# One fp32 kernel on one core: the last two thirds of its instruction order written out as a list, some low halves moved to VectorE, the first loads reordered

## Chip, cores, metric

One core of a Trainium2 chip. The metric is the device time of one execution in microseconds. Engines are named as in the profile: PE is TensorE's matmuls, PEld its weight loads, DVE is VectorE, ACT is ScalarE, POOL is GpSimd, SP is SyncE.

## What is computed

The input x is 2 x 3008 x 256. A real part of a two-dimensional Fourier transform is followed by two gated layers, all in fp32.

```python
def _attn_ref(x):
    X = np.fft.fft(x, axis=1)
    X = np.fft.fft(X, axis=2)
    return X.real.astype(np.float32)

def _moe_ref(x, w_in, w_out):            # w_in 256 x 2048, w_out 2048 x 256
    h = x @ w_in
    relu6 = np.clip(h + 3.0, 0.0, 6.0)
    g = h * relu6 / 6.0
    return (g @ w_out).astype(np.float32)

def _moe2_ref(x, w_gate, w_val, w_out, rms_g):   # 256 x 1536, 256 x 1536, 1536 x 256
    rms = np.sqrt(np.mean(x * x, axis=-1, keepdims=True) + 1e-06)
    xn = x / rms * rms_g
    g = xn @ w_gate
    silu = g * (1.0 / (1.0 + np.exp(-g)))
    val = xn @ w_val
    return (silu * val @ w_out).astype(np.float32)
```

The weights arrive on the device as 64-bit words and are decoded there.

## The kernel before

**Arithmetic.** TensorE works in a format with fewer bits than fp32, so each operand is split into a high half (a copy by ScalarE, which rounds) and a low half (the difference, by `sub` at line 184, on POOL throughout). A product is three matmuls (`PASSES`): high x high, high x low, low x high.

**Transform.** For batch 0 the input is loaded in three pieces (`load_x`, tiles J0, J1, B0), folded by symmetry with sums and differences on VectorE (`sums`, `parts`, `fold`; low halves on POOL), and multiplied with cosine and sine matrices that are loaded as fp16 pairs (`load_raw`) and cast (`conv_mat`). `pmm` and `xmm` are these matmuls (378 columns), `evac` and `evac_x` take the result to the tiles PQX0 and X1, partly by DMA. Batch 1 is folded later (`late_fold`), split (`late_split`), given its matrices by DMAs on POOL's queue (`late_mat`) and multiplied in four groups (`group`) while layer 1 runs. The transform along the 256 columns is multiplied into layer 1's weights: `dec_win` decodes a chunk of w_in and `wmm` multiplies it with `dmat`; `dec_wout` decodes a chunk of w_out. `split_pq` makes the high and low halves of a block of 502 columns of the data.

**Layer 1** is 96 items (6 blocks of 502 columns, 16 chunks of the hidden size; `item1`). An item has eight steps, each on one engine:

1. TensorE, 6 matmuls into two PSUM banks E and O (line 449), out of two pairs of banks that rotate;
2. VectorE, one operation on E (line 453);
3. VectorE, two operations, E + t and t - O (455, 456);
4. ScalarE, two relus (461);
5. VectorE, two operations that read both banks for the last time (464);
6. ScalarE, the high half (467), tiles HI0 and HI1 in turn;
7. POOL, the low half, 128 x 1004 (185), tiles LO0 and LO1 in turn;
8. TensorE, 12 matmuls into four accumulator banks (481); the last of a block adds a step that takes them to a y1 tile.

**Layer 2** is 144 items (12 half blocks of 502 columns, 12 chunks): `in2` with 12 matmuls (608), a sigmoid on ScalarE (610) and two products on VectorE (612, 613); `mid2` with the high half on ScalarE (619) and the low half on POOL; `out2` with 6 matmuls (632). Ahead of a half block stand the RMS steps (`rms_steps`: a square on ScalarE, some fifteen operations on VectorE with three Newton steps, two matmuls). Its weights are loaded in 18 halves (`load_w2`), decoded by one operation on ScalarE and four on VectorE and split (`conv_w2`, lines 175 to 182 and 528); four halves go to HBM and come back later (`take_w2`).

**Order.** Each engine has one queue and runs it in order. All steps from the loads to layer 1's item 35 stand in a list, `STEPS`: each word names a task (the table `TASKS`) or an item, and each time a word occurs the next step of that task is issued; a yield in the code ends a step. This part stands under `tc.manual_schedule()`, which keeps it as written. From item 36 on a loop (`item`) issues the items with fixed distances, and side tasks at fixed places (`LATE`, `at`); this part is outside `manual_schedule`, so the framework's scheduler may order its instructions.

## Time and profile before

| | |
|---|---|
| median of 3 runs | 1177.63 us (1174.83 to 1177.73) |
| the profiled execution | 1175.49 us, span 1173.7 us |
| mean granted TensorE clock | 0.972 |
| TensorE busy | 1081.5 us (92% of the span), 4572 matmuls |
| VectorE busy | 850.3 us (72%), 1204 instructions |
| ScalarE busy | 500.7 us (43%) |
| POOL busy | 510.1 us (43%) |
| moved by DMA | 47.22 MB, mean 40 GB/s |

The profile is of one execution; matmul ends are modelled, so a busy share of TensorE is not its share of peak speed, and the pace at which matmuls start says more. Busy time counts each engine alone: two engines that are both below full can still hold each other up, and which one does is read stage by stage. A granted clock of 1.00 is 2.4 GHz; the lower level, 1.2 GHz, is 0.50.

### The profile page before, as it was taken

The numbers are of one execution on the slowest core, as the hardware profiler recorded it, in microseconds if no ns is written. First come the engines' busy times: TensorE is split into PE (matmuls) and PEld (weight loads), VectorE is DVE, ScalarE is ACT, GpSimd is POOL, SyncE is SP. The second block draws the span as 40 slices with busy tenths as digits, with TensorE's granted clock in tenths as the row PEclk, the third lists the DMA queues.
The fourth block names the chain that finished last, engine by engine and source line by source line (L and its number), as shares of the span: only waits on it lengthen the run. The fifth ranks groups of instructions, "written<-read, shape, count | busy, mean of one in ns | idle before, by whom it ended". The sixth has DMA issues, their size and how long they took to land.

```text
span 1173.7 us, 12674 instructions
## 1 busy us (share of the span) xinstructions
PE 1081.5 (92%) x4572; PEld 876.8 (75%) x4572; DVE 850.3 (72%) x1204; ACT 500.7 (43%) x754; POOL 510.1 (43%) x311
## 2 busy tenths in 40 slices
PE   4778777889999989988999999999999999999998
...
DMA packets 18896, 47.22 MB, mean 40 GB/s; under 512 B 3914, under 2 KB 6986, under 8 KB 17946
## 3 DMA queue, kind: packets, MB, share of 16 engines
...
## 4 chain that ended last, share of the span: by engine, by line
PE 59%; DVE 25%; issue 6%; ACT 4%; POOL 4%; DMA 2%; SPq 0%; DVEq 0%; POOLq 0%; ACTq 0%
PE acc L632 15%; PE E L608 14%; PE O L608 14%; PE acc L481 10%; DVE R L464 5%; DVE T L453 3%; DVE E L455 2%; PE O L449 2%; PE E L449 2%; DVE O L456 2%; POOL LO L185 1%; ACT R L461 1%; DVE c_p L182 1%; DVE c_p L177 1%; DMA J<-in_x 1%
## 5 line engine op out<-in xcount | busy, mean ns | idle before, releaser
L185 POOL TENSOR_TENSOR LO<-R,HI 128x1004 fp32r<-128x1004 f32 x96 | 233.3, 2435 | 198.3 <-ACT HI L467 189.0
L481 PE MATMUL acc<-HI,B 128*128 128x502 f32 x768 | 256.7, 401 | 4.8 <-ACT YB L496 2.2
L612 DVE TENSOR_TENSOR R<-T,E 128x502 f32<-128x502 f32 x144 | 97.4, 676 | 186.0 <-ACT T L610 183.7
L185 POOL TENSOR_TENSOR HI<-R,HI 128x502 fp32r<-128x502 f32 x87 | 115.3, 1325 | 223.8 <-ACT HI L619 223.1
L481 PEld LDWEIGHTS acc<-HI,B 128*128 128x128 f32 x768 | 149.0, 195 | 38.8 <-ACT YB L496 2.6
L467 ACT CAST HI<-R 128x1004 fp32r<-128x1004 f32 x96 | 99.0, 1033 | 151.9 <-PE acc L481 80.0
L481 PE MATMUL acc<-LO,B 128*128 128x502 f32 x384 | 154.6, 402 | 4.5 <-POOL LO L185 4.4
L608 PE MATMUL E<-J,B 128*128 128x502 f32 x576 | 147.5, 391 | 1.1 <-DVE R L612 1.1
L608 PE MATMUL O<-J,A 128*128 128x502 f32 x576 | 147.5, 390 | 1.0 <-ACT A L528 0.6
L610 ACT ACTIVATE T<-E 128x502 f32<-128x502 f32 x144 | 84.5, 588 | 133.7 <-PE E L608 133.5
L185 POOL TENSOR_TENSOR LO<-R,LO 128x502 fp32r<-128x502 f32 x57 | 76.2, 1337 | 145.9 <-ACT LO L619 145.9
L608 PEld LDWEIGHTS O<-J,A 128*128 128x128 f32 x576 | 108.6, 189 | 24.9 <-DVE R L613 1.2
L449 PE MATMUL E<-J,A 128*128 128x502 f32 x288 | 88.1, 418 | 41.9 <-DVE R L464 32.2
L608 PEld LDWEIGHTS E<-J,B 128*128 128x128 f32 x576 | 108.4, 189 | 24.4 <-DVE R L612 2.0
L613 DVE TENSOR_TENSOR R<-R,O 128x502 f32<-128x502 f32 x144 | 97.2, 676 | 11.3 <-DVE R L612 0.5
L449 PEld LDWEIGHTS E<-J,A 128*128 128x128 f32 x288 | 54.7, 198 | 63.1 <-DVE R L464 42.1
L619 ACT CAST HI<-R 128x502 fp32r<-128x502 f32 x87 | 53.1, 612 | 112.9 <-DVE R L613 112.9
L461 ACT ACTIVATE R<-E,c_three 128x502 f32<-128x502 f32 x96 | 65.3, 680 | 77.5 <-DVE E L455 66.6
L481 PEld LDWEIGHTS acc<-LO,B 128*128 128x128 f32 x384 | 74.8, 195 | 24.7 <-POOL LO L185 9.5
L449 PE MATMUL O<-J,A 128*128 128x502 f32 x288 | 86.7, 412 | 5.0 <-DVE A L233 2.6
L632 PE MATMUL acc<-HI,B 128*128 128x502 f32 x354 | 89.9, 391 | 0.4 <-POOL HI L185 0.4
L464 DVE SCALAR_TENSOR_TENSOR R<-R,E 128x502 f32<-128x502 f32 x96 | 64.5, 672 | 28.2 <-ACT R L461 28.1
...
## 6 DMA issues: line engine op xcount, KB each, us to landing
...
```

Source lines behind the costliest of these rows:

```text
L185: eng.tensor_tensor(o, a, b, op=ALU.subtract)
L449: T.matmul(bk[:, :BL], a[:, lw, eo, fs], j[:, eo, lx], start=(n == 0), stop=(n == 2))
L461: S.activation(x, bk[:, :BL], AF.Relu, bias=c3)
L464: V.scalar_tensor_tensor(x, x, 6.0, bk[:, :BL], op0=ALU.min, op1=ALU.mult)
L467: S.copy(hi, r)
L481: T.matmul(acc[k][:, :BL], w[:, lw, f % 4, d * P:(d + 1) * P], (hi, lo)[lx][:, hf * BL:(hf + 1) * BL], start=(first and n == 0), stop=(las ...
L608: T.matmul(bk[:, :BL], w[:, lw, d, fs], j[:, d, lx], start=(m == 0), stop=(m == 5))
L610: S.activation(s, E[:, :BL], AF.Sigmoid)
L612: V.tensor_tensor(u, s, E[:, :BL], op=ALU.mult)
L613: V.tensor_tensor(u, u, O[:, :BL], op=ALU.mult)
L619: S.copy(hi, u)
L632: T.matmul(acc[d][:, :BL], w[:, lw, f % 4, d * P:(d + 1) * P], hl[lx], start=(f == 0 and m == 0), stop=(f == NF2 - 1 and m == 2))
```

## The change

The list `STEPS` now holds every step of the program, 2451 words against 503, and all of it stands under `manual_schedule`. The loop with its fixed distances is gone, as are `LATE` and the places of side tasks. `conv_w2`, the RMS steps (`rms`) and layer 2's items (`item2`, which joins `in2`, `mid2` and `out2`) are cut into steps of one engine by yields; a word with + is a step of a layer 2 item. The instructions are the same, but for one thing: a word that ends in ' puts the low half of its step on VectorE instead of POOL. There are 19 of those: fold0 once, fold1 and fold2 twice each, dwi0, dwo0, pq00, dwi2, pq02, pq10, and eight of layer 2's weight halves (cw31 to cw71). The first part of the list is written anew as well, with the loads in another order.

```diff
...
 STEPS = """
-    x00 xq x01 raw00 raw01 x00 lwi0 raw02 raw11 x02 fx fold0 one fold0 sx0 fold1 mat00 sx0 fold1 fold1 fold1 fold0 sx0
-    mat01 fold1 mat00 mat01 fold0 fold0 fold1 mat00 X00 X01 fold1 dwi0 sx1 fold0 dwi0 dwi0 mat02 mat02 fold0 X02 dwi0
-    mat01 fold1 mat11 dwi0 lwo0 dm fold0 PQ100 PQ000 PQ001 fold0 fold1 raw10 fold2 lwi1 fold2 fold2 sx1 mat11 dwi0 wt0
-    wt0 PQ101 mat11 sx1 dwo0 fold2 evx0 fold2 fold0 dwo0 fold2 dwo0 fold0 mat02 mat10 wt0 fold2 wt0 PQ102 PQ002 dwo0
-    fold2 mat10 fold2 evx0 dwo0 X10 raw12 wt0 ev00 ev10 dwo0 evx0 wt0 X11 ev00 mat10 wt0 ev10 PQ010 dwi1 wt0 mat12 mat12
-    pq00 dwi1 dwi1 mat12 PQ110 PQ011 PQ111 PQ012 PQ112 wt0 lwi3 lwo1 pq00 dwi1 ev01 ev01 X12 ev11 ev11 0 evx1 dwi1 evx1
-    0 0 dwi1 0 1 0 0 0 dwo1 1 1 wt1 dwi3 1 wt1 2 dwo1 1 1 1 dwo1 wt1 lwi2 wt1 wt1 2 2 2 3 2 wt1 wt1 2 pq01 pq01 dwo1 wt1
-    2 3 evx1 wt1 lwo3 x10 lwo2 g 3 3 0 dwi3 4 3 3 3 4 4 4 1 dwi3 5 4 4 4 5 dwo1 dwo1 5 5 2 6 5 5 5 6 6 6 3 dwi2 7 6 6
-    dwi2 6 7 7 dwi2 7 4 8 7 7 7 8 8 8 5 9 8 dwi2 8 dwi2 8 9 9 9 dwi2 6 10 9 9 dwo2 9 10 10 10 7 7 11 10 10 wt2 10 wt2 11
-    dwo2 11 11 8 wt2 wt2 12 11 dwo2 11 dwi3 11 12 wt2 dwo2 wt2 12 dwi3 12 wt2 9 13 12 12 12 wt2 13 wt2 13 dwi3 13 10 14
...
+    one dm x01 raw11 raw00 g xq x00 x00 raw01 lwi0 raw02 x02 raw10 fold1 fold1 mat11 fold1 fold1 mat00 fx sx0 fold1 sx0
+    fold1' sx0 fold1 fold0 mat00 sx1 fold0 fold1 X00 mat00 fold0 fold1' mat11 fold0 mat11 fold0 sx1 sx1 fold0 mat01 fold0
+    fold0 mat01 fold0 dwi0 X01 mat01 dwi0 fold0 PQ100 mat02 dwi0 mat02 fold0' mat02 X02 dwi0 PQ101 evx0 lwo0 dwi0 fold2
+    lwi1 PQ000 evx0 PQ001 dwi0' mat10 evx0 mat10 fold2 wt0 mat10 x10 fold2 wt0 fold2 dwo0 X10 wt0 dwo0 fold2 X11 wt0 wt0
+    fold2' dwo0 PQ102 fold2 PQ002 ev10 dwo0 fold2 fold2' dwo0 ev10 raw12 wt0 dwo0' PQ010 wt0 dwi1 PQ011 wt0 wt0 ev00 dwi1
+    ev00 mat12 dwi1 PQ110 pq00 dwi1 mat12 PQ111 lwi3 lwi2 mat12 pq00' PQ012 dwi1 lwo3 PQ112 ev01 dwi1 ev01 X12 ev11 lwo1
+    ev11 0 evx1 lwo2 evx1 pq01 1 0 dwi3 evx1 pq01 0 1 0 dwi3 1 0 1 dwi3 wt1 0 1 0 dwi3 1 2 1 0 2 dwo1 2 dwo1 2 wt1 dwo1 1
+    wt1 2 wt1 wt1 dwo1 2 3 wt1 wt1 2 wt1 dwo1 wt1 4 3 3 dwo1 2 4 3 4 dwi2 3 4 dwi2 5 3 4 3 5 6 4 dwi2 4 3 6 5 6 5 4 dwi2 6
+    5 dwi2 6 7 5 dwi2' 5 6 8 7 dwo2 7 dwo2 6 5 7 8 7 8 9 7 dwo2 7 8 6 9 8 9 10 8 dwo2 9 8 7 10 dwo2 9 10 11 7 dwo2 11 9 8
+    11 10 9 lf0 9 11 10 lf0 10 wt2 11 10 lf0 wt2 11 11 10 dwi3 x11 wt2 wt2 wt2 wt2 wt2 wt2 dwi3 12 13 12 12 dwo3 11 wt2 13
+    12 dwo3 12 dwo3 14 12 13 12 14 13 dwo3 12 14 dwo3 lf0 dwo3 14 13 14 wt3 13 lf0 13 14 15 lf1 wt3 14 13 wt3 wt3 15 wt3
...
+    22 23 21 22 21 20 23 pq02 23 pq02' 23 21 22 23 22 22 24 23 25 24 24 23 22 25 24 25 24 25 23 24 25 24 26 23 27 26 25 26
+    24 25 27 26 27 26 25 27 26 27 26 28 27 29 28 27 28 26 29 28 29 28 29 27 28 29 28 30 29 31 30 29 30 28 31 30 31 30 31
+    29 30 31 30 32 31 33 32 31 32 30 33 32 33 32 33 31 32 33 32 34 31 33 35 33 34 32 35 34 35 34 33 35 34 35 34 36 34 35
+    37 36 36 35 34 37 36 37 36 37 35 36 37 36 38 37 39 37 38 38 36 39 38 39 38 39 37 38 39 38 40 39 41 40 39 40 38 41 40
...
+    47 gr01 47 47 48 gr01 47 ls11 gr01 46 48 48 ls11 48 49 lm12 lw00 48 47 49 48 49 48 50 47 50 49 48 50 49 50 49 50 51 49
+    50 52 51 51 50 49 52 51 52 51 52 50 51 52 51 53 52 52 gr11 53 53 53 51 lw01 cw00 53 rms2 cw00 gr11 rms2 54 53 cw00
+    gr11 53 52 cw00 pq11 pq11 55 54 lw10 cw00 54 53 55 54 cw00 55 cw01 54 55 cw01 56 54 55 54 56 57 55 cw01 55 54 57 56 57
+    56 55 cw01 57 56 lw11 cw01 57 56 cw01 58 57 56 59 58 cw10 cw10 57 56 59 58 59 58 57 cw10 59 58 59 58 60 cw10 58 59
...
+    cw40 +3 +4 cw40 +4 +4 cw40 +3 +5 +5 +4 cw40 +5 lw50 cw40 +6 +5 cw40' +5 cw41 cw41 +7 cw41 +6 +6 cw41 +6 lw51 cw41 +5
+    +6 cw41' +7 +6 cw50 +7 +8 cw50 +7 cw50 +7 cw50 +7 +6 +8 lw60 cw50 +8 +9 cw50' +8 cw51 +8 cw51 +8 cw51 +7 +9 +9 +8 cw51
...
-    def sub(eng, o, a, b):
-        eng.tensor_tensor(o, a, b, op=ALU.subtract)
+    low = [G]
+
+    def sub(o, a, b):
+        low[0].tensor_tensor(o, a, b, op=ALU.subtract)
...
-        sub(G, s[:, 1], f, f32(s[:, 0]))
+        sub(s[:, 1], f, f32(s[:, 0]))
...
-    def conv_w2(k, a, direct):
+    def conv_w2(k, a):
+        direct = k == 0 or k >= 3
         key, slot = CH2[k]
         f = sl("c_p9", [P, 512])
-        for _ in decode(rw2.pop((k, a)), f):
-            pass
+        yield from decode(rw2.pop((k, a)), f)
+        yield
...
+    def rms(n):
+        tag = ("W0", "W1")[n] if n < 2 else "R2"
...
+        for _ in range(3):
+            yield
...
-    def in2(i):
+    def item2(i):
...
+        t = sl(HL2[i % 5], [P, 2, BL], F32R)
+        hl = (t[:, 0], t[:, 1])
+        S.copy(hl[0], u)
+        yield
+        sub(hl[1], u, f32(hl[0]))
+        yield
...
-    def item(i):
-        if i < n1:
-            run("item1", i)
-            fifo.append((finish, "item1", i))
-        elif i < total:
-            in2(i - n1)
-            fifo.append((out2, i - n1))
-        if 1 <= i <= n1:
-            run("item1", i - 1, n=3)
-        if i < n1:
-            run("item1", i, n=3)
-        if n1 <= i < total:
-            mid2(i - n1)
-        if len(fifo) > 3 or i >= total:
-            fn, *k = fifo.pop(0)
-            fn(*k)
-
...
+    with tc.manual_schedule():
+        for step in STEPS.split():
+            task = step.rstrip("'")
+            low[0] = V if step != task else G
+            key = TASKS[task] if task in TASKS else ("item2", int(task)) if task[0] == "+" else ("item1", int(task))
+            if key not in live:
+                g = fns[key[0]](*key[1:])
+                live[key] = g if hasattr(g, "__next__") else iter(())
+                if not hasattr(g, "__next__"):
+                    continue
             next(live[key], None)
```

## Rows read from the trace of the kernel before

**Rows 1.** Page, 40 equal slices of the span: TensorE's busy tenths.
```profile
PE   4778777889999989988999999999999999999998
```

**Rows 2.** Windows by stage: PE, PEld, DVE, ACT, POOL busy (count), clock, DMA, GB/s.
```profile
0.00:53.50 53.50, 31.44 (x120) 27.89 (x121) 40.94 (x65) 30.92 (x43) 18.70 (x14) 0.90 0.71 219
53.50:248.20 194.70, 154.12 (x579) 118.97 (x578) 154.86 (x210) 90.28 (x124) 94.14 (x42) 0.89 0.16 48
248.20:563.10 314.90, 292.56 (x1242) 232.74 (x1241) 276.71 (x401) 169.90 (x239) 186.71 (x98) 0.98 0.17 46
563.10:668.80 105.70, 102.54 (x444) 82.75 (x443) 87.51 (x120) 47.79 (x80) 49.94 (x36) 1.00 0.19 55
```

**Rows 3.** The same view, 8-item windows of layer 1, 24 items of layer 2.
```profile
94.70:152.70 58.00, 42.43 (x158) 32.73 (x156) 38.63 (x53) 26.14 (x36) 25.79 (x11) 0.88 0.01 0
365.50:403.40 37.90, 34.82 (x144) 26.62 (x145) 37.76 (x53) 21.20 (x30) 20.89 (x11) 1.00 0.13 43
447.80:478.80 31.00, 31.00 (x137) 25.62 (x136) 25.50 (x42) 18.78 (x25) 19.05 (x9) 1.00 0.00 1
518.30:563.10 44.80, 37.68 (x148) 27.45 (x147) 44.77 (x61) 20.21 (x28) 22.17 (x9) 0.96 0.08 24
668.80:767.80 99.00, 99.00 (x436) 81.99 (x435) 61.77 (x88) 32.66 (x55) 32.31 (x25) 1.00 0.03 11
```

**Rows 4.** Waits from 53.5 to 248.2 us: total us, times, longest.
```profile
DVE R L464 <- ACT R L461: 23.1, 19, 6.5
DVE A L233 <- ACT A L231: 6.4, 2, 5.6
ACT HI L467 <- PE acc L481: 62.5, 19, 9.9
PE E L449 <- DVE R L464: 20.0, 9, 4.2
```

**Rows 5.** Timelines of VectorE and POOL: start us, us, engine, line, operation.
```profile
455.41 0.73 DVE L453 SCALAR_TENSOR_TENSOR T<-X,c_wx,E 128x502 f32<-128x502 f32 x1
456.06 0.67 DVE L464 SCALAR_TENSOR_TENSOR R<-R,E 128x502 f32<-128x502 f32 x1
412.14 0.42 DVE L177 TENSOR_SCALAR c_p<-c_p 128x512 f32<-128x512 f32 x1
412.59 2.46 DVE L178 TENSOR_SCALAR c_p<-c_p 128x512 int32<-128x512 int32 x1
412.20 5.08 POOL L185 TENSOR_TENSOR LO<-R,HI 128x1004 fp32r<-128x1004 f32 x2 [1.22 <-ACT HI L467]
```

**Rows 6.** Groups by form, VectorE, 53.5 to 563.1 us: busy us, mean ns.
```profile
L177 DVE TENSOR_SCALAR c_p<-c_p 128x512 f32<-128x512 f32 x7 | 8.5, 1216 | 0.0
L178 DVE TENSOR_SCALAR c_p<-c_p 128x512 int32<-128x512 int32 x7 | 9.7, 1379 | 0.1
L180 DVE SCALAR_TENSOR_TENSOR c_p<-W,c_p 128x512 int32<-128x512 int32 x7 | 7.3, 1045 | 0.0
L182 DVE SCALAR_TENSOR_TENSOR c_p<-W,c_p 128x512 int32<-128x512 int32 x7 | 9.6, 1367 | 0.0
```

**Rows 7.** Groups by form, whole span: low halves on POOL and differences on VectorE.
```profile
L185 POOL TENSOR_TENSOR YB<-B,YB 126x512 fp32r<-126x512 f32 x6 | 8.7, 1442 | 7.3 <-ACT YB L273 7.3
L185 POOL TENSOR_TENSOR B<-W,B 128x1024 fp32r<-128x1024 f32 x5 | 11.9, 2381 | 4.9 <-ACT B L203 3.5 <-ACT B L417 1.3
L233 DVE TENSOR_TENSOR A<-acc,A 128x512 fp32r<-128x512 f32 x2 | 1.4, 688 | 0.8 <-ACT A L231 0.8
L585 DVE TENSOR_TENSOR J<-LO,J 128x1004 fp32r<-128x1004 f32 x12 | 14.4, 1197 | 0.6 <-ACT J L584 0.6
```

**Rows 8.** Timeline of VectorE in the first 56 us.
```profile
14.79 1.45 DVE L249 TENSOR_TENSOR H<-J 126x512 f32<-126x512 f32 x1 [2.02 <-DMA J<-in_x]
18.21 0.75 DVE L260 TENSOR_TENSOR J<-H 126x256 f32<-126x256 f32 x2
25.00 4.04 DVE L260 TENSOR_TENSOR J<-H 126x256 f32<-126x256 f32 x2
```

More of the change, by code (lines that the diff above doesn't have):

```diff
@@ L38 @@
 TASKS = {
[L39 removed]
[19 rows of a table removed]
[26 rows of a table added]
+    "mat10": ("conv_mat", 1, 0), "mat11": ("conv_mat", 1, 1), "mat12": ("conv_mat", 1, 2), "one": ("consts",),
[10 rows of a table added]
 }
 STEPS = """
[L61 to L63 removed]
@@ L418, in dec_wout @@
         yield
[L419 removed]
+        sub(tl, f, f32(th))
     jit = {}
@@ new lines, in rms @@
+        y = y1[blk][:, :, cs]
+        sq = sl(tag, [P, 2, BL])
+        S.activation(sq, y, AF.Square)
+        yield
+        sm = sq[:, 0]
+        V.tensor_tensor(sm, sm, sq[:, 1], op=ALU.add)
+        yield
+        hl = sl("LO2", [P, 2, BL], F32R)
+        V.tensor_copy(hl[:, 0], sm)
+        yield
+        V.tensor_tensor(hl[:, 1], sm, f32(hl[:, 0]), op=ALU.subtract)
+        yield
+        p = bank(io()[0])
+        for i in range(2):
+            T.matmul(p[:, :BL], ones, hl[:, i], start=(i == 0), stop=(i == 1))
@@ L590, in fft_mlp_mlp_kernel @@
+        for d in range(2):
+            yield
+            V.scalar_tensor_tensor(xn[:, d], y1[blk][:, d, cs], gsc[:, d:d + 1], r, op0=ALU.mult, op1=ALU.mult)
+        yield
+        t = sl(f"J{(n + 1) % 2}", [P, 2, 2, BL], F32R)
+        S.copy(t[:, :, 0], xn)
+        yield
+        V.tensor_tensor(t[:, :, 1], xn, f32(t[:, :, 0]), op=ALU.subtract)
+        jit[2, n] = t
     p2 = {}
@@ L653, in load_g @@
         SY.dma_start(gsc, rms_g)
-    n1 = NB * NQ * NF1
-    n2 = 2 * NB * NQ * NF2
-    total = n1 + n2
-    fifo = []
     fns = {k: v for k, v in locals().items() if callable(v)}
     live = {}
-    def run(name, *arg, n=1):
-        key = (name, *arg)
-        if key not in live:
-            g = fns[name](*arg)
-            live[key] = g if hasattr(g, "__next__") else iter(())
-            if not hasattr(g, "__next__"):
-                return
-        for _ in range(n):
-            next(live[key], None)
```

188 lines of the change are left out of this document (83 added, 105 removed), and 62 rows, old and new, of tables (STEPS, TASKS).

## The prediction

> **What bounds the kernel now.** I read four views, in this order. First the slices of the page: TensorE's digit is 7 or 8 in most of the first quarter of the span and 9 without a break only from slice 20 (557 us) on [rows 1]. Then busy times by stage, with edges at the first matmul of layer 1's item 0 (53.5 us) and item 32 (248.2), of layer 2's item 0 (563.1) and item 24 (668.8) [rows 2]. I call the stretches A to E. In E a matmul of 502 columns starts every 0.227 us (99.0 us for 436 [rows 3]): nothing is left there but to run it. In D 444 matmuls x 0.227 = 101 of 105.7 us. In C 1242 x 0.227 = 282 (an upper value, 72 of them are shorter) of 314.9, VectorE 276.7. In B 579 x 0.227 = 131 of 194.7, VectorE 154.9, so 40 us in which VectorE does nothing although it has the most work. A is 53.5 us with VectorE busy 40.9. So against TensorE's own pace B loses 64 us, C 33 and D 5; E loses nothing.
>
> Third, inside C by eight items: the planned-late work (decoding layer 2's weights, the RMS steps) makes VectorE full in some blocks (37.76 of 37.90 us, 44.77 of 44.80) while TensorE starves, and in another the reverse (31.00 of 31.00 for TensorE, 25.50 for VectorE) [rows 3]; C runs at whichever engine is fuller. B does not: in its items 8 to 15 VectorE is busy 38.63 and TensorE's 158 matmuls need 35.9 of 58.00 us [rows 3]. Fourth, the waits of B tell why: VectorE waits 23.1 us for the relu of ScalarE and 6.4 us for its cast in wmm, ScalarE waits 62.5 us for output matmuls that free the HI buffers, TensorE 20.0 us for VectorE's last step on a bank [rows 4]. It is a ring of in-order queues, none of which is full, and the granted clock is 0.89 there against 1.00 in D [rows 2], a mean over 1.2 and 2.4 GHz.
>
> **VectorE's prices.** An item of layer 1 gives VectorE one step at 0.65 us from start to start (455.41 to 456.06) and four at about 0.585, so 3.0 us [rows 5]; TensorE needs 18 x 0.227 = 4.1. An operation of VectorE that has SBUF operands alone is another matter: L177 took 0.42 us while POOL was idle, L178, of the same form, 2.46 us when it started after POOL's L185 had [rows 5]. In C the four decode lines take 1.22, 1.38, 1.05 and 1.37 us [rows 6]; the first two forms take 0.42 when free [rows 5], the other two I put at 0.68 (the free price of a 502-wide two-operand instruction, close to L233's 0.69 [rows 7]). That is 0.80 + 0.96 + 0.37 + 0.69 = 2.8 us of waiting for POOL in four instructions, 0.70 each. The Trainium skill (SBUF — State Buffer, "Who interferes with whom") says that VectorE and GpSimd share one pair of ports as an exclusive lock, held for a whole instruction; the two rows agree.
>
> **The change, part by part.** *Low halves.* 19 go from POOL to VectorE: in A five of the folds (512 wide), dwi0, dwo0 (1024) and pq00 (1004); in B dwi2 and pq02; in C pq10; then eight 512-wide ones of layer 2's weights. POOL loses 1.44 and 2.38 us for a narrow and a wide one; VectorE takes 0.69 and, by the 1004-wide L585, 1.20 [rows 7]. In A that is 5 x 0.69 + 3 x 1.20 = 7.1 us on the fuller engine. POOL keeps two low halves there, so VectorE's collisions go: two L260 took 4.04 us behind POOL and 0.75 us free, the first L249 at 14.79 took 1.45 [rows 8]; I take 5 us back (between 0 and 7). The eight late ones cost 8 x 0.69 = 5.5 us of VectorE under a TensorE that is full (VectorE 87.5 of 105.7 and 61 of 99): nothing, and 5.5 if that cover were gone. The Trainium skill (Perfetto Trace Analysis, "Optimizing Scalar/DVE Operations") warns that moving work between VectorE and GpSimd may not help because they share a port; by it alone the moved halves in A to C would bring nothing back and A to C would cost their whole 10.7 us, which I have as the upper bound of the term.
>
> *Loads.* SP now starts with x01 (1008 KB in one piece) and raw11, with dm on POOL's queue beside them and g and xq behind them; before it was half of x00, xq, x01. VectorE's first sums start later but find x01 whole, whereas before it waited 2.02 us for the second half of x00 [rows 8]. I take +1 us (from -3 to +4). Later x10, lwi2, lwi3, lwo1 to lwo3 stand ahead of item 0; x10 waits on SP for the last cast of mat10 (slot PQ1), and behind it queue raw12, the row of wt0 and the copies of evx0, for which mat12 and item 0's first VectorE step wait. The last mat10 cast stands just ahead of x10 in the list, so I put nothing on it. **A: 53.5 + 7.1 - 5 + 1 = 56.5 us** (50 to 63).
>
> *The order in B.* A number in the list is the next step of that item: 1 input matmuls, 2 and 3 VectorE, 4 relu (ScalarE), 5 VectorE (frees the banks), 6 cast to HI (ScalarE), 7 low half, 8 output matmuls. Counting in the two lists, for items 0 to 31, how many other steps VectorE has between steps 3 and 5 of one item: before none in 16 items and one in 16; after none in 0, one in 4, two or more in 28. And the relu stands directly behind another item's HI cast, the one that waits for TensorE, in 23 of 32 before and in 13 after. So the 23.1 + 6.4 us that VectorE waits in B [rows 4] lose their cause, mostly. VectorE's work there grows by 6 us: two wide low halves (2.4) and the last two steps of lf2 (2 x 2 x 0.96). It can't go below 154.9 + 6 = 161 plus some 9 us in items 24 to 31, where the new list leaves VectorE 24 us beside TensorE's 33: 170. If all the stalls stayed it would be 194.7 + 6 + 9 = 210. I take the value nearer the lower end, since the rows name ScalarE as the cause and the list answers just that: idle 39.8 - 24.5 (five sixths of 29.5) = 15, **B: 161 + 15 = 176 us.**
>
> *C, D, E.* In C the new list runs items in pairs (in 32, in 33, out 30, out 31), with the same seven halves of layer 2's weights, both first RMS rows and four late groups in it, and again bunched in items 48 to 71 and 80 to 95. VectorE's sum changes by pq10's 1.2 and lf2's -3.8: less than 3 us. Neither engine's sum shrinks, so **C: 315 us** (290 to 350, by what VectorE waits for POOL, below). D has 5 us to give beside TensorE's 101; I take 2: **103.5**. **E: 505.** The RMS steps of layer 2, now single and spread, lie under full TensorE; so do loads and stores.
>
> Sum: 56.5 + 176 + 315 + 103.5 + 505 = 1156 us, against the span of 1173.7. The profiled execution was 1175.5, 1.8 above its span, and the median of the three runs, 1177.6, another 2.1 above that. So 1156 + 3.9 = **1160 us**, 1.5% faster.
>
> **The rivals.** *Behind POOL (slower).* Place: C, where VectorE is full. With pairs, POOL runs two low halves of 2.4 us one behind the other (a pair took 5.08 [rows 5]), and the 19 new instructions on VectorE are of the kind that waits. C holds about 70 such instructions (28 of decodes, some 34 of RMS, 8 of late folds), which wait 0.70 us each now. If they wait half a POOL instruction, 1.2 us, that is 70 x 0.5 = 35 us: 1160 + 35 = 1195. It decides from 0.25 us more per instruction (17.5 / 70). For it: VectorE has no slack in two of the blocks of C shown [rows 3], and every step's place is now fixed for all of the program, whereas the rest of C ran close to its fuller engine before. Against: POOL's total in C is the same.
>
> *Port freed (faster).* The same 70 instructions find POOL idle more often, because they are placed in smaller pieces: half of 70 x 0.70 = 25 us off C: 1135. The Trainium skill (Perfetto Trace Analysis, "Optimization Strategy") speaks for such interleaving of stretches with different limits. The trace shows those stretches [rows 3]; it shows no order that avoids POOL.
>
> *Given back (no change).* B ends earlier, but VectorE's whole work up to the end of layer 1 is what counts: it grows by 7 us, and weights that arrive or are decoded at the old times hold layer 2's first items. Then A and C take what B gives: 1177.
>
> **How the numbers follow.** Forecast 0.54, behind POOL 0.25, port freed 0.13, given back 0.08. The forecast's own range, with A from 50 to 63, B from 170 to 190 and D from 101 to 106, is 1145 to 1183. The range with the rivals: down to 1125 (port freed with B at its lower end of 170 and A at 53), up to 1197 (behind POOL, with A 2 us worse). What a measurement of this kernel can tell from no change is about 0.3%, 3.5 us. Faster: the forecast but for its upper end (0.51) and port freed (0.13), 0.64. Same: given back and a sliver of the forecast, 0.09. Slower: 0.27.
>
> **What would show it.** Right: item 32's first matmul at about 232 us, VectorE's wait for L461 between items 0 and 31 under 8 us, the granted clock there above 0.93; item 0 at 55 to 57 with L260 near 0.4 us each; layer 2's first matmul near 548. Wrong: item 32 at 250 or later (the ring has moved, not gone); the decode lines of C above 1.6 us in the mean (behind POOL) or below 0.9 (port freed); VectorE idle over 15 us in A (the loads). The stretch E must stay at 99 us for 24 items; if it does not, the list itself has starved TensorE, and all of the above is beside the point.

## The result, and the profile after

The kernel after took 1141.59 us in the median of its runs (1141.25 to 1142.43), the kernel before 1176.23 in the same comparison (1173.40 to 1177.73): a ratio of 0.9709, with a 95% interval from 0.9687 to 0.9732. The change is 2.9% faster; the forecast was 1160 us, 1.5% faster, with a range from 1125 to 1197.

First the windows by stage of the kernel after, the view of [rows 2]; the edges are item 0's first matmul, item 32's, layer 2's first and its item 24's.

```profile
0.00:55.30 55.30, 29.26 (x121) 25.86 (x122) 40.06 (x73) 31.94 (x44) 4.56 (x7) 0.91 0.70 232
55.30:231.50 176.20, 149.63 (x589) 116.14 (x588) 160.22 (x222) 92.71 (x127) 93.72 (x44) 0.93 0.20 53
231.50:533.80 302.30, 287.33 (x1241) 233.05 (x1240) 255.97 (x389) 168.99 (x235) 181.66 (x94) 0.99 0.16 42
533.80:636.20 102.40, 100.80 (x435) 81.50 (x434) 90.60 (x130) 47.53 (x79) 39.09 (x27) 1.00 0.20 62
```

Against [rows 2] A is 1.8 us longer (55.3), B 18.5 shorter (176.2), C 12.6 shorter (302.3), D 3.3 shorter (102.4), and E, from there to the end, 504.4 against 504.9. The span went from 1173.7 to 1140.7 us. TensorE's matmuls are the same. Of the 33.0 us, 19 are time in which it had none; the other 14 are busy time (1081.5 us before, 1067.5 now), at a mean granted clock of 0.98 instead of 0.97. VectorE is busy 5 us longer in B, and 20.7 us less in C with nearly the same work. The windows don't hold quite the same matmuls, as the new list issues an item's outputs earlier: 12 more start in B, 8 fewer in D. Priced as in the prediction, at 0.227 us for 502 columns, TensorE needs 133.7 us in B, 277.4 in C and 98.5 in D, where it needed 130.9, 277.4 and 100.3. Above that B loses 42.5 us where it lost 63.8, C 24.9 where it lost 37.5, D 3.9 where it lost 5.4. I call a comparison of such losses one at like work.

The waits of B, from 55.4 to 231 us, against [rows 4] (L547 is L464 of before, L544 the relu 461, L550 the HI cast 467, L564 the outputs 481):

```profile
PE E L532 <- DVE R L547: 12.9, 8, 3.1
...
ACT HI L550 <- PE acc L564: 8.6, 4, 3.2
...
DVE R L547 <- ACT R L544: 0.5, 1, 0.5
```

VectorE's 23.1 us for the relu are 0.5, and ScalarE's 62.5 for the output matmuls are 8.6. TensorE's 20.0 us for VectorE at the items' inputs are 12.9.

In C the window of items 88 to 95, and that of 24 items of layer 2, against [rows 3] (whose fourth and fifth rows are these):

```profile
493.00:533.80 40.80, 39.85 (x171) 31.58 (x170) 35.80 (x59) 21.83 (x30) 24.94 (x11) 1.00 0.05 21
636.20:730.30 94.10, 94.10 (x414) 77.89 (x414) 59.52 (x87) 32.39 (x53) 32.16 (x24) 1.00 0.03 12
```

Items 88 to 95 took 44.80 us with VectorE busy 44.77; now 40.80 and 35.80. Not every block gained: items 56 to 63 took 37.90 us [rows 3] and now take 40.30. The last row holds 414 matmuls in 94.1 us, the same 0.227 each as before.

The decode lines of C, against [rows 6]:

```profile
L261 DVE SCALAR_TENSOR_TENSOR c_p<-W,c_p 128x512 int32<-128x512 int32 x7 | 8.7, 1249 | 0.0
...
L259 DVE TENSOR_SCALAR c_p<-c_p 128x512 int32<-128x512 int32 x7 | 7.1, 1009 | 0.2
L258 DVE TENSOR_SCALAR c_p<-c_p 128x512 f32<-128x512 f32 x7 | 6.5, 933 | 3.0 <-ACT c_p L256 3.0
...
L263 DVE SCALAR_TENSOR_TENSOR c_p<-W,c_p 128x512 int32<-128x512 int32 x7 | 5.3, 758 | 0.0
```

The four decode lines were 5.01 us together, now 3.95 (0.93 + 1.01 + 1.25 + 0.76): a mean of 0.99 us for an instruction where it was 1.25.

In A the eight differences of the folds, some of which waited behind POOL at [rows 8], are L343 now; one of its rows, VectorE's wait for x after, and its waits for inputs before:

```profile
19.55 1.23 DVE L343 TENSOR_TENSOR J<-H 126x256 f32<-126x256 f32 x3
```
```profile
DVE H L332 <- DMA J<-in_x: 5.7, 1, 5.7
```
```profile
DVE c_xq L323 <- DMA c_xq<-in_xq: 4.9, 1, 4.9
...
DVE H L249 <- DMA J<-in_x: 2.8, 2, 2.0
```

Each takes 0.41 us (1.23 for three). VectorE waits 6.4 us for inputs in all (0.7 of it for xq), where it waited 7.7; the 2.02 of [rows 8] are only the longest wait of the before for a piece of x.

### The profile page after: what moved, and what is told of

Read it like the earlier page. It is cut to its first block, busy times and chain, and to the rows that moved or that the text cites. A ratio compares the mean times of both kernels' runs of the same rounds, so it can differ in the third digit from the quotient of the medians.

```text
span 1140.7 us, 12657 instructions
## 1 busy us (share of the span) xinstructions
PE 1067.5 (94%) x4572; PEld 870.2 (76%) x4572; DVE 832.6 (73%) x1223; ACT 504.8 (44%) x754; POOL 483.0 (42%) x292
## 4 chain that ended last, share of the span: by engine, by line
PE 70%; DVE 21%; issue 3%; DMA 3%; ACT 1%; POOL 1%; SPq 0%; DVEq 0%; ACTq 0%; POOLq 0%
PE acc L709 16%; PE E L687 16%; PE O L687 16%; PE acc L564 13%; DVE R L547 4%; PE E L532 3%; PE O L532 3%; DVE T L536 2%; DVE O L539 2%; DVE E L538 2%; DMA J<-in_x 1%; PE E L435 1%; PE O L435 1%; POOL LO L268 1%; DVE c_p L258 1%
## 5 line engine op out<-in xcount | busy, mean ns | idle before, releaser
L564 PE MATMUL acc<-HI,B 128*128 128x502 f32 x768 | 250.9, 394 | 0.1
L268 POOL TENSOR_TENSOR HI<-R,HI 128x502 fp32r<-128x502 f32 x87 | 119.0, 1367 | 239.0 <-ACT HI L699 238.9
L564 PEld LDWEIGHTS acc<-HI,B 128*128 128x128 f32 x768 | 147.0, 191 | 30.6 <-ACT HI L550 0.5
L564 PE MATMUL acc<-LO,B 128*128 128x502 f32 x384 | 153.5, 400 | 10.5 <-POOL LO L268 10.3
L687 PE MATMUL E<-J,B 128*128 128x502 f32 x576 | 147.3, 391 | 0.0
L687 PE MATMUL O<-J,A 128*128 128x502 f32 x576 | 146.6, 389 | 0.0
L550 ACT CAST HI<-R 128x1004 fp32r<-128x1004 f32 x96 | 99.2, 1034 | 97.6 <-DVE R L547 63.2
L687 PEld LDWEIGHTS E<-J,B 128*128 128x128 f32 x576 | 108.9, 189 | 22.9
L687 PEld LDWEIGHTS O<-J,A 128*128 128x128 f32 x576 | 108.8, 189 | 22.5
L544 ACT ACTIVATE R<-E,c_three 128x502 f32<-128x502 f32 x96 | 65.4, 682 | 97.7 <-DVE E L538 78.9
L564 PEld LDWEIGHTS acc<-LO,B 128*128 128x128 f32 x384 | 73.5, 191 | 34.4 <-POOL LO L268 19.7
L709 PE MATMUL acc<-HI,B 128*128 128x502 f32 x354 | 90.5, 391 | 0.0
L532 PE MATMUL O<-J,A 128*128 128x502 f32 x288 | 85.2, 406 | 0.0
L709 PEld LDWEIGHTS acc<-HI,B 128*128 128x128 f32 x354 | 66.8, 189 | 14.4 <-POOL HI L268 0.4
```

The lines of the kernel that those rows point to most:

```text
L268: low[0].tensor_tensor(o, a, b, op=ALU.subtract)
L532: T.matmul(bk[:, :BL], a[:, lw, eo, fs], j[:, eo, lx], start=(n == 0), stop=(n == 2))
L544: S.activation(x, bk[:, :BL], AF.Relu, bias=c3)
L550: S.copy(hi, r)
L564: T.matmul(acc[k][:, :BL], w[:, lw, f % 4, d * P:(d + 1) * P], (hi, lo)[lx][:, hf * BL:(hf + 1) * BL], start=(first and n == 0), stop=(las ...
L687: T.matmul(bk[:, :BL], w[:, lw, d, fs], j[:, d, lx], start=(m == 0), stop=(m == 5))
```

## The experiments

All times in us. C, D and E as above, B in two parts; "before" is the median of the kernel before over the experiments' comparisons (1177 to 1178). In the diffs a word of the list is written as item/step, and words of decodes and late folds that stand between are left out, except where the diff is of them.

| kernel | time | ratio to before | A | B, 0 to 23 | B, 24 to 31 | C | D |
|---|---|---|---|---|---|---|---|
| before | 1177.5 | 1 | 53.5 | 152.8 | 41.9 | 314.9 | 105.7 |
| after | 1141.6 | 0.971 | 55.3 | 143.3 | 32.9 | 302.3 | 102.4 |
| e_head | 1166.5 | 0.990 (0.988-0.993) | 53.5 | 152.6 | 42.0 | 309.6 | 102.7 |
| e_tail | 1150.6 | 0.977 (0.975-0.979) | 56.3 | 143.4 | 32.9 | 307.0 | 105.6 |
| e_headA | 1144.1 | 0.972 (0.969-0.974) | 53.2 | 147.5 | 32.9 | 302.6 | 102.4 |
| e_avorder | 1144.3 | 0.971 (0.969-0.973) | 55.4 | 142.4 | 35.6 | 302.4 | 102.7 |
| e_bact | 1176.6 | 0.999 (0.997-1.000) | 53.1 | 152.6 | 41.1 | 314.6 | 105.7 |
| e_aact | 1139.5 | 0.968 (0.966-0.970) | 55.1 | 139.3 | 34.1 | 302.4 | 102.2 |
| e_bout | 1168.4 | 0.992 (0.990-0.994) | 52.3 | 147.4 | 42.0 | 314.8 | 105.2 |
| e_bactout | 1173.1 | 0.997 (0.995-0.999) | 52.3 | 151.3 | 41.0 | 314.8 | 105.7 |
| e_bwt | 1169.5 | 0.994 (0.992-0.996) | 54.5 | 147.3 | 41.9 | 314.9 | 105.1 |
| e_bwtout | 1165.6 | 0.990 (0.988-0.993) | 53.8 | 141.7 | 42.3 | 315.1 | 105.6 |
| e_awt | 1144.0 | 0.972 (0.969-0.975) | 54.6 | 143.2 | 32.9 | 302.3 | 102.6 |
| e_bplace | 1182.6 | 1.004 (1.003-1.006) | 52.6 | 170.0 | 34.5 | 311.4 | 105.2 |
| e_aplace | 1152.3 | 0.979 (0.977-0.981) | 54.6 | 140.2 | 40.0 | 309.2 | 102.3 |
| e_bplwo | 1169.9 | 0.995 (0.993-0.997) | 55.1 | 156.0 | 34.5 | 313.0 | 105.6 |
| e_bnoread | 1133.0 | 0.962 (0.960-0.965) | 52.4 | 145.5 | 35.6 | 287.0 | 105.2 |
| e_anoread | 1108.6 | 0.942 (0.940-0.944) | 57.7 | 128.3 | 32.9 | 284.4 | 101.6 |
| e_nolow | 1149.8 | 0.977 (0.974-0.979) | 57.7 | 143.4 | 32.9 | 303.3 | 106.5 |
| e_aactout | 1145.8 | 0.974 (0.972-0.975) | 56.0 | 144.6 | 34.1 | 302.4 | 102.5 |

E is 503.9 to 505.5 in all of them. A moves by 3 us between kernels that have the same A (52.3 to 55.1 for the old list, 54.6 to 57.7 for the new, the last in e_anoread, whose edit doesn't touch A), so no less than that is read from it.

### Which part of the list gives what

The first three join the two lists: e_head runs the old first part (loads to item 35), then the new order of the rest; e_headA the old list up to item 0 only; e_tail the new list up to item 36, then the old loop.

```diff
# e_head, e_headA, on the list of the kernel after
-STEPS = (new list)
+STEPS = (old list, whole or up to item 0) + (words of the new list not yet used, in its order)
# e_tail, on the kernel before
-STEPS = (old list)
+STEPS = (new list up to the first step of item 36)
```

> The list of the kernel before up to its end (its loads, its folds, items 0 to 35 in its order, no low half on VectorE), then the rest of the new list. Theory 1 (what the order within items 32 to 95 gains is its own): item 32 starts at about 248 us as before, items 32 to 95 then take 302 to 306 us as in the changed kernel, and the time is 1141.6 + 18.5 - 1.8 = 1158 us. Rival (the 12.6 us of items 32 to 95 come from late folds and loads that the new list does earlier): they take 315 us as before, 1171 us.

> The new list up to the word that starts item 36, then the loop of the kernel before, reordered by the framework. Theory 1: item 32 at 231 us as in the changed kernel, items 32 to 95 at 313 to 317 us as before, the first 24 items of layer 2 at 105: 1141.6 + 12.6 + 3.3 = 1157 us. Rival (as above): items 32 to 95 at 303 us, 1145 us.

> The list of the kernel before up to item 0 (its loads and folds, all low halves there on POOL), then the rest of the new list. Theory 1 (the stage up to item 0 is worth the 1.8 us by which it got longer): item 0 at 53.5 us, 1140 us. Rival (the new first part pays later, by loads that are in earlier): item 0 at 53.5 us but items 0 to 31 longer than 176 us, 1146 us or more.

e_head gains 11.6 us of its own: C 5.3, D 3.0, E 1.1, and about 2 in which the timed runs differ from the profiled one. e_tail gains 27: B all of its 18.5, and C 7.9 with the old loop. At like work C's gain is 8.0 us in e_head and 5.1 in e_tail. So the 12.6 us of C come from two sides, the order of the rest and work that the first part has done earlier. The traces show where, when C is cut at item 48; before, after and e_head, items 32 to 47 and 48 to 95, columns as above:

```profile
248.20:330.20 82.00, 78.75 (x354) 65.24 (x353) 61.18 (x99) 42.48 (x60) 54.36 (x38) 1.00 0.30 61
330.20:563.10 232.90, 213.81 (x890) 167.50 (x889) 215.53 (x302) 127.42 (x180) 132.35 (x61) 0.98 0.13 40
```
```profile
231.50:306.60 75.10, 75.10 (x343) 63.53 (x342) 55.97 (x89) 41.04 (x56) 48.52 (x31) 1.00 0.23 47
306.60:533.80 227.20, 212.23 (x900) 169.52 (x899) 200.00 (x300) 127.94 (x179) 133.14 (x64) 0.98 0.14 40
```
```profile
248.10:330.40 82.30, 78.81 (x356) 65.70 (x355) 62.99 (x100) 44.06 (x61) 52.91 (x36) 1.00 0.29 56
330.40:557.70 227.30, 212.06 (x900) 169.51 (x899) 200.43 (x300) 127.74 (x179) 133.56 (x64) 0.98 0.14 40
```

TensorE needs 77.1 and 200.3 us for these stretches in the kernel before, 74.6 and 202.8 after, 77.3 and 202.8 in e_head. So the kernel before loses 5.0 and 32.5 us in them, the kernel after 0.5 and 24.4, e_head 5.0 and 24.5: the 4.5 us in items 32 to 47 need the new first part, the 8.1 in items 48 to 95 come with the new order of the rest alone. e_headA is nearer its rival: with the old list up to item 0, A is 53.2 us against 55.3, but items 0 to 23 take 4.2 more, and the time is 1144.1. The new first part pays in B, not in A.

### VectorE's spacing and ScalarE's order

e_avorder puts VectorE's step 5 back behind its own step 3 in items 0 to 31: no other step of VectorE, or one, lies between them in 29 of 32 items, as before in 32, where the new list has two or more in 28. e_bact puts the relu ahead of the HI cast in the old list, e_aact behind it in the new one.

```diff
# e_avorder, items 20 and 21
-21/1 20/2 20/3 21/2 18/8 20/4 21/3 19/7 20/5 22/1
+21/1 20/2 20/3 18/8 20/4 19/7 20/5 21/2 21/3 22/1
# e_bact, items 20 and 21
-21/1 20/5 20/6 20/7 21/2 21/3 21/4 18/8
+21/1 20/5 21/2 21/3 21/4 20/6 20/7 18/8
# e_aact, items 5 and 6
-4/8 6/4 5/5 6/5 7/1 5/6 5/7
+4/8 5/5 7/1 5/6 6/4 6/5 5/7
```

> The changed kernel; in items 0 to 31 alone, steps 2 and 3 of other items that VectorE does between steps 3 and 5 of an item are put behind its step 5, so that 5 follows 3 with none or one step between in 29 of 32 items, as in the kernel before. Theory 1 (that spacing is what items 0 to 31 gained by): VectorE waits about 20 us for the relu again, items 0 to 31 take 190 to 200 us and the time is 1155 to 1162 us. Rival (the gain there comes from the order of the matmuls and of the HI casts): under 1146 us.

> The kernel before with one order changed, ScalarE's: in items 0 to 32 the relu of an item stands ahead of the HI cast of the item before it, not behind it. VectorE's and TensorE's orders stay. If the relu behind a cast that waits for output matmuls is what held VectorE in B (step 4 behind step 6), B falls from 194.7 us to between 176 and 184, the wait of VectorE for the relu (23.1 us) to under 8, and the time to 1160-1168 us beside 1178. If the place of the weights' transposing matmuls on TensorE alone is the cause, B stays above 190 and the time above 1173.

> The kernel after with one order changed, ScalarE's: in items 1 to 31 the relu stands behind the HI cast of the item before it, as in the kernel before. If that order is the cause, B rises from 176.2 us to 185-195 and the time from 1141.6 to 1150-1160. If it only matters where wmm stands ahead of outputs (which the new list does not have), B stays within 4 us and the time within 1138-1147.

Neither order alone is the cause; both undone together were not run. e_avorder has 178.0 us in B, 1.8 more than after. e_bact has 193.6, e_aact 173.4 and is not to be told from after in the whole time. The waits of e_bact in B, VectorE's and ScalarE's:

```profile
DVE R L464 <- ACT R L461: 15.9, 17, 4.8
```
```profile
ACT R L461 <- POOL LO L185: 40.8, 18, 2.6
ACT HI L467 <- PE acc L481: 8.4, 4, 2.8
```

The wait that was to go did go: the HI cast waits 8.4 us for TensorE, not 62.5. In its place the relu, now early, waits 40.8 us for POOL, whose low half still reads the R buffer that the relu writes. One link of the ring took over from another, and VectorE's wait for the relu only fell from 23.1 to 15.9.

### wmm between the items

VectorE's longest idle times of the kernel before, of 6.5, 5.6 and 5.0 us, lie about items 11, 18 and 13, beside wmm (chunks 2 and 3). The timeline there, before:

```profile
113.11 2.93 PE L222 MATMUL E<-YB,LO 128*128 128x512 f32 x6 [3.06 <-DVE R L464]
...
115.83 2.76 PE L222 MATMUL O<-YB,LO 128*128 128x512 f32 x6
...
121.65 1.03 ACT L467 CAST HI<-R 128x1004 fp32r<-128x1004 f32 x1 [6.90 <-PE acc L481]
...
123.29 0.68 DVE L464 SCALAR_TENSOR_TENSOR R<-R,E 128x502 f32<-128x502 f32 x1 [6.50 <-ACT R L461]
```
```profile
133.25 0.69 DVE L233 TENSOR_TENSOR A<-O,A 128x512 fp32r<-128x512 f32 x1
```

wmm takes the pair of banks that item 10 gave back, and 12 matmuls of it stand on TensorE ahead of the outputs of item 8. The HI cast of item 10 waits for those outputs (6.90 us), the relu of item 11 stands behind the cast, VectorE waits 6.50 for the relu, and wmm's pair comes free only when its last low half ends at 133.94, 20.8 us after its first matmul; until then the items have one pair. The granted clock from 113.1 to 133.9 is 0.83. After, the pair is held from 118.11 to 125.85, 7.7 us, at 1.00, behind the outputs of item 9.

e_bout moves three output steps ahead (items 0, 8, 15), e_bwt bunches wmm's casts and low halves, e_bwtout does both; e_bactout is e_bout with e_bact; e_awt spreads wmm in the kernel after.

```diff
# e_bout, chunk 3 (chunks 1 and 2 alike)
-14/8 wt3/1 18/1 wt3/2 17/5 17/6 wt3/3 wt3/4 17/7 18/2 18/3 18/4 15/8
+14/8 15/8 wt3/1 18/1 wt3/2 17/5 17/6 wt3/3 wt3/4 17/7 18/2 18/3 18/4
# e_bwt, chunk 3
-wt3/3 wt3/4 17/7 18/2 18/3 18/4 15/8 wt3/5 wt3/6 19/1 18/5 wt3/7 18/6 wt3/8
+wt3/3 wt3/4 wt3/5 wt3/6 wt3/7 wt3/8 17/7 18/2 18/3 18/4 15/8 19/1 18/5 18/6
# e_awt, chunk 2
-wt2/3 wt2/4 wt2/5 wt2/6 wt2/7 wt2/8 12/1 13/1 12/2 12/3 11/8
+wt2/3 wt2/4 12/1 12/2 12/3 wt2/5 wt2/6 wt2/7 wt2/8 13/1 11/8
```

> The kernel before with three words moved: the output matmuls of items 0, 8 and 15 stand ahead of those of the next item or of wmm (chunks 1, 2, 3), so that TensorE doesn't run 12 wmm matmuls, and wait for a pair of banks for them, before the outputs that the HI cast waits for. ScalarE's and VectorE's orders stay. If wmm's place ahead of the outputs is the cause of B's large stalls (about 29 of its 35 us of VectorE gaps lie in items 2, 3, 11 to 13, 18 and 19, around wmm), B falls to 178-186 us and the time to 1162-1170. If ScalarE's order alone is the cause, B stays above 190.

> Both edits of the last two, the relu ahead of the cast and the outputs ahead of wmm. If the two links are one ring, breaking both gives hardly more than breaking one: B 174-182, time 1156-1166 us, within 4 us of the better of the two. If they are separate causes the gains add, and B goes to 172 or below.

> The kernel before with wmm's casts and low halves (steps 5 to 8 of chunks 2 and 3, 6 to 8 of chunk 1) directly behind the step before them, not spread over one to two items, so that the pair of banks that wmm takes from the items goes back sooner. If holding that pair (20.8 and 18.8 us) is the cause of B's stalls, the hold falls to under 13 us, VectorE's gaps at items 11 to 13 and 18 to 19 (24 us) shrink by half, B falls from 194.7 to 180-187 us and the time to 1163-1170. If not, B stays above 190.

> The last edit and, with it, the outputs of items 0, 8 and 15 ahead of the next item's or of wmm's matmuls, which alone brought 9 us of the whole time. If the hold of the banks is what both shorten, the two together give B 176-184 and 1158-1167 us. If the hold is no cause, it equals the outputs alone: B 189, 1168.

> The kernel after with the reverse: wmm's casts and low halves of chunk 2 moved behind item 12's VectorE steps 2 and 3, ahead of item 13's input matmuls, and the last two of chunk 3 to just ahead of item 16's. If the hold of the banks is the cause, it grows from 7.7 and 10.8 us to 12 or more each, B from 176.2 to 182-190 us and the time from 1141.6 to 1147-1156. If not, B stays within 3 us.

In the old order wmm's place is worth 11 us: items 0 to 23 go from 152.8 to 141.7 with both edits, 147.4 and 147.3 with one each. One edit alone stayed short of what was expected of it (B 189.3 in both), and the two add up. The relu's order with e_bout (e_bactout) undoes its gain, 151.3, which neither theory had; why is not shown. e_awt misses too: the hold grew to 10.1 and 15.3 us, where 12 or more each were meant, and nothing changed in B. So a longer hold costs nothing in the new order, while in the old one a shorter hold gains 5.5 us with the outputs behind wmm and 5.7 with them ahead. What makes this difference is open.

### Where the other work stands

e_bplace and e_aplace exchange the places of the decodes, late folds and halves of layer 1's x in items 0 to 35 between the two lists; the items' steps and wmm stay. e_bplwo is e_bplace with the two edits of e_bwtout.

```diff
# e_bplace, on the list before (lf2, the last late fold, as an example)
-17/2 17/3 17/4 14/8 wt3/1 ... 28/4 25/8 29/1 lf2/2 28/5
+17/2 lf2/1 17/3 17/4 lf2/2 14/8 wt3/1 ... 28/4 25/8 29/1 28/5
# e_aplace, on the list after
-22/4 21/7 20/8 23/2
+22/4 21/7 lf1/2 20/8 23/2
```

> The kernel before with the items' own steps and wmm's where they were, but the other work of items 0 to 35 (decodes, late folds, halves of layer 1's x) at the item where the new list has it: late folds at items 11 to 20 instead of 17 to 32, decodes of dwi3 and dwo1 earlier or later by some items. If the place of this work is the cause of B's gain (it fills VectorE's idle 19.4 us of items 8 to 15 and leaves items 24 to 31 to TensorE, 41.9 us before against 32.9 after), B falls from 194.7 to 180-187 us and the time to 1160-1169. If the interleaving of the items two by two is the cause, B stays above 190 and the time above 1172.

> The kernel after with the reverse: items two by two and wmm as they are, the decodes, late folds and halves of items 0 to 35 at the item where the kernel before has them. If the place of this work is the cause, B rises from 176.2 to 186-196 us and the time from 1141.6 to 1150-1162. If the items' interleaving is, B stays within 4 us and the time below 1147.

> The kernel before, items one by one, with the decodes and late folds at the new list's items (as in e_bplace) and with wmm's casts bunched and outputs ahead of it (as in e_bwtout). If wmm was what kept the late folds from fitting into VectorE's idle time, items 0 to 23 take 144-152 us and items 24 to 31 33-35: B 178-186, time 1157-1166 us. If they fit only where the items run two by two, the two edits add up: items 0 to 23 156-162, B 190-196, time 1168-1176.

Windows of B, items 0 to 23 and 24 to 31, columns as above, of before, after and e_bplace, and the first of e_bplwo:

```profile
53.50:206.30 152.80, 117.28 (x434) 89.60 (x432) 115.60 (x157) 68.87 (x94) 71.41 (x32) 0.88 0.19 54
206.30:248.20 41.90, 36.84 (x145) 29.37 (x146) 39.26 (x54) 21.41 (x30) 22.73 (x10) 0.92 0.07 25
```
```profile
55.30:198.60 143.30, 116.73 (x445) 89.07 (x444) 134.80 (x182) 72.43 (x99) 74.19 (x35) 0.92 0.24 65
198.60:231.50 32.90, 32.90 (x145) 27.07 (x144) 25.42 (x41) 20.28 (x29) 19.54 (x9) 1.00 0.00 1
```
```profile
52.60:222.60 170.00, 124.48 (x434) 94.69 (x433) 128.65 (x177) 69.94 (x96) 72.73 (x34) 0.81 0.20 57
222.60:257.20 34.60, 33.21 (x146) 27.14 (x145) 25.55 (x41) 20.40 (x29) 20.98 (x9) 1.00 0.00 1
```
```profile
55.10:211.10 156.00, 120.82 (x434) 93.31 (x434) 127.70 (x177) 70.30 (x96) 74.79 (x34) 0.86 0.22 62
```

Items 24 to 31 are settled, from both sides: without the late folds they take 32.9 to 35.6 us, with them 40.0 to 42.3. Nine of B's 18.5 us are this. Much of it is VectorE waiting behind POOL: its instructions there took 7.5 us more than the shortest of their line and shape in the kernel before, 0.5 after, and in e_bnoread (below), where POOL only fills, the same items take 35.6 us with the folds among them. Items 32 to 47 belong to this as well: the kernel after takes 75.1 us for them, e_aplace, with the same matmuls, 82.1. The work has to go somewhere, and there the lists part: in the old order the new places cost items 0 to 23 17.2 us (152.8 to 170.0, granted clock 0.81), in the new one 3.1 (140.2 to 143.3). wmm's two edits take 14.0 of that off (156.0). Of the other 12.7 to after's 143.3, 4.2 go with the list up to item 0 (e_headA, 147.5), and 8.5 stay open, or 11.3 at like work, since the new order's window holds 2.8 us more of matmuls. What is left that differs is the items' own order, two by two, with the next item's input matmuls issued ahead of VectorE's first step on this one; VectorE's spacing and ScalarE's order, each alone, are excluded above. So neither theory of e_bplace and e_aplace holds whole: by the first the place of the work is no cause (B 204.5), by the second B keeps 14 of its 18 us under the old places, but the time is 10.7 longer, C 6.9 of that. e_bplwo came out as expected of two edits that add up.

### POOL and the low halves

e_bnoread and e_anoread let POOL write zeros where it made the low half of layer 1's products; e_nolow takes the mark off all 19 words, so that POOL makes every low half.

```diff
# e_bnoread (e_anoread alike)
-        sub(G, lo, r, f32(hi))
+        G.memset(f32(lo), 0.0)
# e_nolow
-fold1' sx0 fold1 fold0 mat00
+fold1 sx0 fold1 fold0 mat00
```

> The kernel before with POOL's low half of each layer 1 item replaced by a fill with zero: leaves out the low half of layer 1's products, so that POOL reads nothing there and is shorter. If VectorE's waiting behind POOL (41.9 us in C over the free durations) is what C pays in the kernel before, C falls from 314.9 to 285-300 us, and further than it does in the kernel after with the same edit; B falls too, by up to 20. If C is set by the order of the items and TensorE's queue, C stays within 5 us.

> The kernel after with the same edit (leaves out the low half of layer 1's products). If the new list's gain in C (302.3 against 314.9 us) is less waiting behind POOL (23.0 against 41.9 us in VectorE), C falls here to 285-298, to within 5 us of the kernel before with the same edit. If it is something else, C keeps a lead of 8 us or more on the kernel before with the same edit.

> The kernel after with all 19 low halves back on POOL and every step at its place. By the prediction they cost 7.1 us on VectorE in A and give 5 back, cost 2.4 in B, 1.2 in C and nothing later: time within 4 us of 1141.6, A 53 to 57. If moving them is what takes VectorE's waiting behind POOL out (0.3 us left in A of 7.3), the time is above 1147 and A above 58.

The decode lines of e_bnoread in C, what POOL ran there, and the windows of items 32 to 47 and 48 to 95 of e_bnoread and e_anoread:

```profile
L180 DVE SCALAR_TENSOR_TENSOR c_p<-W,c_p 128x512 int32<-128x512 int32 x7 | 6.6, 942 | 0.0
L177 DVE TENSOR_SCALAR c_p<-c_p 128x512 f32<-128x512 f32 x7 | 5.2, 737 | 1.5 <-ACT c_p L175 1.5
L182 DVE SCALAR_TENSOR_TENSOR c_p<-W,c_p 128x512 int32<-128x512 int32 x7 | 4.8, 682 | 0.0
...
L178 DVE TENSOR_SCALAR c_p<-c_p 128x512 int32<-128x512 int32 x7 | 3.2, 452 | 0.0
```
```profile
L470 POOL MEMSET LO<- 128x1004 f32 x65 | 61.0, 939 | 174.1 <-PE acc L481 174.1
```
```profile
233.50:313.00 79.50, 78.47 (x357) 66.19 (x356) 59.43 (x99) 43.85 (x63) 31.39 (x39) 1.00 0.32 63
313.00:520.50 207.50, 203.20 (x885) 165.57 (x885) 187.07 (x304) 125.66 (x177) 60.26 (x61) 1.00 0.14 45
```
```profile
218.90:293.80 74.90, 74.90 (x343) 63.57 (x342) 56.25 (x89) 41.04 (x56) 25.43 (x30) 1.00 0.24 47
293.80:503.20 209.40, 206.29 (x900) 168.37 (x899) 181.95 (x300) 127.80 (x179) 62.88 (x64) 1.00 0.15 44
```

The four decode lines fall from 5.01 us together to 2.81 when POOL only fills (0.94 us each, 65 of them). C falls to 287.0 and 284.4, so of the 12.6 us between the two kernels 2.6 are left. At like work the lead of the new list is 1.3 us in items 32 to 47, where it was 4.5, and 1.3 in items 48 to 95, where it was 8.1.

Summed over items 48 to 95, VectorE's instructions took 38.6 us more than the shortest one of the same line and shape in the kernel before, 22.5 after, 22.9 in e_head, 7.9 and 5.1 in these two; at those shortest durations the work of the kernels before and after is nearly the same, 199 and 197 us. (Over all of C the two have 41.9 and about 23 us.) So the new order from item 48 on takes 16 us of VectorE's waiting behind POOL away, and the time there is 8.1 us shorter at like work. As both kernels come close to TensorE's need of 277 us for C in these runs, the runs alone would not tell waiting from any other load of VectorE; the durations do. One rival is left: a fill is also 1.5 us shorter than a low half and doesn't wait for the HI cast, so that part of what these two runs gain can be POOL's own. In items 32 to 47 it must be more than waiting, since VectorE's durations were only 3.3 us above their shortest there before, and 1.2 after.

The low halves by themselves are worth 8 us (1149.8 against 1141.6), where I had expected none to speak of. The place to look is A, and D, where TensorE waits for POOL's low halves; A's window of e_nolow, and D's wait, e_nolow first, then after:

```profile
0.00:57.70 57.70, 28.98 (x120) 25.58 (x121) 41.34 (x65) 32.23 (x44) 19.00 (x15) 0.91 0.69 225
```
```profile
PE acc L710 <- POOL LO L269: 2.8, 3, 1.2
```
```profile
PE acc L709 <- POOL LO L268: 0.9, 1, 0.9
```

In A, VectorE is busy 41.34 us with 65 instructions and 40.06 with 73: the eight that came cost 7.0 us at their free durations and took 7.5 of waiting away, since POOL is busy 4.56 us there and not 19.0. What the stage gains by it isn't shown: 57.7 us without them, 55.3 with them, but also 57.7 in e_anoread, which has them. D is 4.1 us shorter, of which 1.9 stand in the wait shown; C is 1.0 shorter.

### A version to beat both

> The kernel after with ScalarE's order of e_aact (1139.5 us) and, with it, wmm's matmuls of chunk 3 behind the outputs of item 13. VectorE waits 3.1 us for TensorE at item 15, behind wmm, in the kernel after. If that wait is wmm's place, up to 3 us come off: 1136.5-1139.5 us. If it only moves, 1139-1142.

```diff
# on e_aact
-15/1 wt3/2 14/7 13/8 wt3/3 wt3/4
+15/1 14/7 13/8 wt3/1 wt3/2 wt3/3 wt3/4
```

It lost 6 us to e_aact, nearly all in items 0 to 23 (144.6 against 139.3), where both theories had a gain or nothing. It puts outputs ahead of wmm, the move that gains 5 in the old list, though item 15's inputs come ahead of wmm with them. The best kernel measured that leaves nothing out is e_aact, 1139.5 us (1139.08 to 1141.66); its ratio overlaps with that of after.

## Why the prediction was right or wrong

**The size.** The sum was 1156 for a span of 1140.7. Of the 15.4 us by which the stages miss, C is 12.7, A 1.2, D 1.1, E 0.6, B -0.2. The term that failed is C: "Neither engine's sum shrinks, so C: 315 us". It measured 302.3, and the runs show two things in its place.

The larger is 8.1 us at like work in items 48 to 95. VectorE's sum did shrink there (215.5 to 200.0), because 38.6 us of its durations were no work but waiting for POOL, and 22.5 are now. e_head shows that the new order from item 36 on does it (22.9). The working had that price, 0.70 us for each of some 70 instructions, and the rival "port freed" took half of it, 25 us, off C. Its mechanism was at work, but 16 us of waiting went and, with it, 8 us of time; that all of the 8 are due to it is argued from the durations.

The other is 4.5 us in items 32 to 47. The term counted the last late folds, which left C there, only as VectorE's 3.8 us less, and took "less than 3 us" in all as nothing. In the kernel before TensorE lost 5.0 us in these items although VectorE was busy in only 61 of 82 us, so that it was not an engine's sum that held them. Without the late folds and halves TensorE is full there (75.1 of 75.1 us). e_head, which keeps the old first part, has none of this gain, and e_aplace loses it again.

The signs that I set on the decode lines, above 1.6 and below 0.9, both stayed out: 0.99. One reading of the price was loose: L177 at 412.14 was not free of POOL, its 0.42 us began 0.06 before POOL's pair.

**B: the right number for a wrong reason, by luck.** 176 was forecast and 176.2 came, with VectorE's wait for the relu at 0.5 us and the clock at 0.93, just at the bound that I set. But the counts from which the term was worked out, how many steps lie between VectorE's steps 3 and 5 and how often the relu stands behind a cast, are not the cause: undone one by one, they move B by 1.8 and -2.8 us (e_avorder, e_aact). The row said that VectorE waits for ScalarE [rows 4]; it did not say why ScalarE was late, and the step from the one to the other skipped TensorE. Shown in their place: the late folds out of items 24 to 31 (9 us), and, in the old order, wmm and its outputs (11 to 14). For items 0 to 23 of the new order 8.5 us, 11.3 at like work, have no cause that is shown. The "9 us in items 24 to 31" that I added as a cost of the new list, because VectorE would idle there, is no cost but the place of the gain: 41.9 to 32.9, TensorE's own pace.

**The low halves.** The price, 7.1 us in A, was right (7.0). Taking 5 back was low (7.5), so that a cost of 2.1 us was forecast where VectorE's busy time fell by 1.3. In D nothing was wrong with "nothing" for their cost, but their worth was left out: 4.1 us (e_nolow), 1.9 of them in TensorE's wait for POOL's low halves. The Trainium skill (Perfetto Trace Analysis, "Optimizing Scalar/DVE Operations") warns that moving work between VectorE and GpSimd may not help as they share a port; here it did, by 8 us (e_nolow), with half of it in D.

**The loads.** I had 1 us more of waiting for them; VectorE waits 6.4 us for inputs in A where it waited 7.7. A came to 55.3 for 56.5. VectorE's idle time there, 15.2 us, is just past the 15 that I set as a sign of wrong loads, but the loads are not why it grew from 12.6: its longest wait for ScalarE there went from 3.0 to 4.8 us.

**The rest.** E is as forecast, D 1.1 us shorter. "Behind POOL" did not come true, though POOL does run two low halves in a row; "given back" neither: C took nothing of B's gain, it gained from it (e_tail, 5.1 us at like work with the old loop, 3.0 of them in items 32 to 47, since late folds and their halves were out of its way).
